# v of block 0 loaded in 1 KB runs and put in token order by 0/1 matrix products, with a new order table

## The chip, the core and the metric

The kernel runs on one NeuronCore of a Trainium2 chip. Five engines work at the same time, each through its own list of instructions in order: TensorE (matrix products; PE in the profile, PEld its weight loads), VectorE (DVE), ScalarE (ACT), GpSimd (POOL) and SyncE (SP), which only issues transfers. Transfers run on 16 DMA engines. TensorE writes to PSUM, eight banks of 128 x 512 fp32 values; the other engines read results from there. The metric is the device time in microseconds. Before the change it is 293.98 us, the median of three runs (293.78 to 295.15).

## The reference

Chunked attention, then a bilinear feed-forward part:

```python
# q, k, v: (8 batches, 8 heads, 576 tokens, 64), chunks of 64 tokens
scores = q_c @ k_c.T / sqrt(64)          # inside each chunk
attn   = softmax(scores)                 # (sum + 1e-9 below)
out    = attn @ v_c
x = out.transpose(0, 2, 1, 3).reshape(4608, 512)
y = ((x @ w_a) * (x @ w_b)) @ w_out      # 512 -> 1536 -> 512
```

Inputs and output are fp32. The kernel computes its products in bf16 and accumulates in fp32.

## The kernel before

The 4608 tokens are nine blocks of 512; a block is two units of 256 tokens. For each unit the kernel loads q, k and v, casts them to bf16, turns q and k so that the head dimension lies on the partitions, forms scores, the exponential E (ScalarE), its sums (products with ones), the inverse of the sums, and the values, and multiplies the two into `xT`, x with features on the partitions. The feed-forward part then streams `xT` past the weights. For block 0 that is `ffn`, 24 groups of four products of 128x512 (L772), each group one tile of 128 hidden features of w_b or w_a. From block 1 on it is `side_group` (L861) and `out_seven` (L1166, and L1004 at the end), which need fewer products through sums and differences of operands.

Block 0 is special, because everything waits for it. Its q and k are loaded by head pairs (`load_pair`): pair m is heads 2m and 2m+1, all 512 tokens, and partition p takes four tokens in a row, so that a run in memory is 4 x 64 x 4 bytes = 1 KB. `cast_pair` casts, `turn_pair` turns a pair's q or k with four products and copies the result to `qkT` so that tokens are in order; `scores_pair`, `sums_pair` and `values_pair` follow. `sums_pair` makes the inverse of the sums with two VectorE reciprocals for pair 1 and with ScalarE's Ln and Exp for the others. v of block 0 is loaded by `load_v0` with tokens on the partitions in order: a run is one head of one token, 256 B. Two loads make a half (256 tokens, all heads), and `cast_v` casts a half to the buffer `vb` in one instruction of 128x1024. `values_pair` reads both `vb` buffers. The same scheme with pairs serves units 2 and 3 (block 1); the later units use loads of another shape and turns by DMA.

The weights w_a and w_b come in pieces of 512 KB (`load_four`), each half of the input features for 512 hidden features, and are cast to `WA` and `WB`. The groups of the first four tiles of each weight are split, so that their first half can start with the first half of the input features (xT of pairs 0 and 1).

The order of all work is written out by hand in a table, `ORDER_OF_ALL`, which `Planner.follow` reads: each word is an engine letter (a TensorE, b ScalarE, c VectorE, d GpSimd, e a DMA issue) with the number of an operation and, behind a colon, the PSUM banks that it takes. A word with f is a filler, one 128x512 product of a zero tile into a free bank (L1474 in the profile). Per engine, instructions stand in the table's order. One extra rule holds for GpSimd: its instruction waits for the last VectorE instruction of a fast kind ahead of it in the table.

The end of the kernel writes the groups' results by DMA; nothing of it is touched except for its place in the table.

Of the kernel before, what the change touches and what calls it, by code (L numbers as in the profile page):

```python
# [85 lines left out]
c113 e0 b1 e2 b3 e4 e8 b5 e6 e9 c48 f0 f1 f2 f3 f4 f5 f6 f7 f0 f1 a49:0 c50 d51 f2 a52:1 d57 f3 f4 a58:2 b7  # L86
d60 e10 e11 f5 a61:3 d66 b62 c53 a54:45 c59 f6 f7 a63:67 e12 b55 b56 a67:0 c68 b64 b65 f1 f2 a93:12 d69 a70:3
b71 f4 f5 f6 a72:45 c94 b73 a86:67 b74 b75 b88 d78 a79:0 b80 f3 f3 f4 a76:3 b77 f5 f1 f4 f5 a81:45 a99:17 b87
c84 c95 d85 a96:03 c97 f6 a90:62 b89 c91 d13 e16 d17 e135 e14 d15 c98 e18 e134 e20 e22 b83 b101 b82 f5 a106:50
b108 a103:74 a110:63 b100 e115 c92 b107 b109 c112 d145 c111 a158:2 a170:0 b102 c105 c104 a152:1 a153:5 a171:3  # L90
a164:6 a165:4 a166 c168 a159:7 a154 b19 a160 a161 c162 e133 e114 a155 d21 c23 c246 b156 c248 c250 a146:6 b147
a172 b123 b174 a173 c175 a188:1 b190 b120 a180:2 a184:6 b186 a167 a176:0 e28 a124:1 b139 a140:3 b141 d142
a143:6 b182 b144 c157 d29 e30 c31 a200:5 c125 c169 e117 d129 a130:1 e116 a121:3 c163 b178 b131 d126 a127:2
b128 a204:4 e136 e24 d148 a149:6 b150 c122 c25 c258 e26 c27 c252 c247 c254 c256 b206 b202 a196:7 a208:03 b210
b209 e137 a227:12 b228 b229 a181:6 c183 c198 a192:4 b194 a185:5 c187 e138 e32 a220:30 a271:12 a177:4 e34 d33
c35 c179 a189:6 c191 d249 e119 e118 c132 a193:7 a205:5 c260 b222 d253 b151 a224:04 b221 b223 c225 c226 d285
b273 b272 b274 a275:36 c276 e36 b37 a201:2 a197:1 c277 c283 c284 c195 a287:0 b288 a289:4 b290 a333:3 c334
a341:6 c207 a336 b337 d251 d255 d257 d286 e44 e38 a338 b339 d39 e263 b45 c199 a331:7 c332 c203 a342 a340:3
b343 a382:5 a351:1 a345 c344 e42 e262 e40 d41 b346 c347 a349:7 b350 a353 b354 a362:2 c363 a355 a359 c360 a357
c358 b43 a364:0 a372:2 b352 c365 a369 d268 e46 c230 a367 b47 c238 c242 a411:6 b370 a376 c377 c378 b368 a373  # L100
d231 d243 c356 e265 e264 b269 a412 b374 a371:3 c375 a384 b413 b385 c233 c232 c239 c241 c234 c244 c240 e214
b383 e213 b218 a423:0 a390 a424 c391 e211 e212 b217 d335 a388 c389 a393:4 a380:7 b381 a426 a427 e216 b428 a400
a398 a431 a395:2 a386 b401 a432 a407 c237 e266 e267 b279 c236 a429:3 d235 c425 b433 c394 c387 e270 b399
a308:04 b310 c396 b408 b309 a404 a430 a443 a320:12 b405 b321 a416 b322 d366 c348 a444 a414 c245 c361 c259 c261
c397 c434 c379 c453 a324:40 c445 e219 a280:12 b323 c325 a446 a447 c326 c448 a402:6 c406 b281 b282 a300:41 b302
b301 b303 e215 d278 a304:20 d435 c392 e292 e312 e291 a403:3 c409 d410 a418 c419 d457 c305 c306 a535:1 a420
c421 c436 c438 b415 b297 a526:4 a587:6 a536 a441:7 b442 a439:2 b440 a519:0 c520 d437 a524 b525 c417 e293 e294
d298 a517:3 a522 b523 c518 a531 b532 a527:0 c533 b537 a528 b529 c530 e311 a561:5 b562 b317 a579:3 a540 a544
a538 c545 c580 a584 c539 a542 c543 c541 e449 e314 e313 b318 a559:0 d422 d463 d521 b585 a577:3 a591 d459 c461
b560 c578 a582 b583 b592 c593 a597:2 c598 d454 d462 d534 d458 a612:4 a586:7 a588 b589 c590 d594 a595:3 b596  # L110
a605 c606 a599 c600 a619 e315 a601 a603 c604 c602 d456 d464 e465 e296 e467 a617 a614:6 a547:0 a548 b618 d455
b620 e316 b327 e299 a328:75 a623 a626 b330 b329 c615 a550 b627 e472 e319 a488:65 b489 b490 e466 c613 c624
a480:47 b482 c549 a638 c639 a640 c641 a551 c552 e295 d546 a622:0 b481 b483 a506:65 a510:37 b508 d307 a484:42
a555 c628 d616 e493 c486 c485 a621:5 c625 c629 c460 b507 e451 e498 e496 e468 a553:2 e494 e469 e452 e501 e471
b509 c512 c511 c630 c631 a753:6 a644 a693:4 a556 b557 e470 a636:7 a642 c643 e495 b477 e492 c645 d575 a554
a634:3 b637 a563 c632 d607 e474 a698 a564 b699 c635 a696 b565 c694 c558 c697 a691:5 a705 d646 c581 c692 d573
c574 a700:0 a701:4 a702 a566 a733:1 b706 c707 b478 b703 a712 e491 e450 b503 e497 b504 a567 c704 e500 a735:5
d633 a718 a716 b713 d608 e475 e476 e502 e473 c568 b487 a709:2 a760:3 c736 a758 c754 c719 b759 a710 b711 d647
d648 d650 a751:6 d609 c717 a714 c734 a756 c752 b757 c715 c720 a761:4 a765 b766 c767 a769:0 a762 a721:6 a771:7
a722 c763 a773 c764 a777 e499 e652 c723 d610 e651 e479 b772 b657 a779 a775 b774 c778 a793 b770 a791 e505  # L120
a668:61 d755 c780 c794 b670 a514:34 a724 a725 a800 b516 b515 a660:14 d768 d708 d611 c649 c792 c776 d781 c695
b669 a680:36 b681 b661 b682 b662 c726 e571 a788:5 c789 a797 b801 a786:3 a729 c787 c798 d513 a664:15 a684:64
b683 c685 c686 a730 b663 a814 a796:3 a812 a795:6 a727:4 a728 e572 e656 e672 e671 b677 c665 c666 a810:1 a825:5
d804 c805 e674 b731 b813 e673 e653 b678 c802 b811 a808:0 a818 c799 d576 d803 a737 a832 a738 a816 e654 b658
c809 c826 c790 c819 d782 c815 c817 c820 c806 a902:5 a830 e570 b739 e655 b833 a827:3 c828 a834:2 a835:7 b831
a836 b837 c732 a839 c840 c841 e676 e675 b687 a900:6 c838 d807 a846 a740 d749 c747 d748 b903 a925:3 a852 c853
a850 c851 a932 b901 a930 c926 c933 d667 d784 b931 b847 a741 c742 a848 c849 a936 a934:7 b937 c938 e679 a865:23
b870 e659 e858 a688:04 b689 b690 a947 c783 d829 c948 a939 e855 a927:1 c928 c940 a935:3 c941 a864:04 d750 b869
a892:62 b896 b895 a951 a943:1 c952 e885 e884 e882 c944 b867 b866 b868 a945:2 a843:6 c946 a949 c950 a844 a953
c954 b845 a962:4 d821 d889 c963 c822 a970:7 a967 c968 a891:05 a914:34 c929 b897 c917 c823 d942 e886 c916 c893  # L130
c978 a965 b966 a874 a875 b876 e887 b920 e856 a960:4 a974 e883 b888 c975 c976 c894 d842 c961 e857 b862 a969:3
a871:0 a872 a879 a971 b972 c973 a984:5 a880 a992 a986 c985 d955 d854 d979 a877:4 a1006 a878 c987 e569 e745
c873 b861 e860 d980 a990 e859 e1059 c993 c991 e746 c1007 a982:1 b983 d981 d898 a1074:0 c824 a1001:7 c1002
a1004 a988 a999:3 c1000 b881 d785 a904 a1008:7 b1005 a1010 a905 a1009:3 b1011 c956 e744 a1013 b1014 c899 a907
a1020 a908 d964 c989 c977 c994 c995 d957 a1103:2 c1012 a1024 d996 b1021 c1015 a1026 c1075 c1104 b906 a1076:1
b1077 d921 c1025 a1108 a1105:6 b1109 a1110 c1027 b1111 c909 a1022 c1023 e890 a1039:27 b1044 c1106 e1030 e1031
e743 e863 a915:34 b918 b1043 b919 a1114 c1115 a1112:5 c1116 a1117 c1118 a1121:7 a1066:63 b1070 b1069 c1122
a1038:24 b1040 a1125 c1126 b1041 b1042 a1129 e1029 e1034 d998 e1032 c1130 e1056 d923 d922 d1003 a1138:3 c1139
e1057 e1058 e1060 c1036 a1127 a1113:6 c1128 a1092:20 b1035 c1016 a1065:45 c1067 a1017:3 a1143 a1123:1 a1018
a1045:4 c1119 b1071 c1095 c1124 c1094 d1062 b1019 b1144 a1131 a1140:0 e912 c1132 a1149 a1046 c1150 e1033 e910  # L140
e1210 e1061 e1235 b1072 e1209 a1048 a1049 b1050 e913 a1147:2 a1145 b1146 c1068 a1164 c1047 c1141 d959 d958
d1156 d997 a1053 e1208 c1157 e1212 c1107 c1159 c1158 c1120 b1063 a1054 b1055 c1165 a1152 b1153 a1148:6 c1154
a1160:5 a1051:4 a1162:0 c1151 b1161 d1028 d924 a1170 c1171 a1168 c1169 a1179:7 a1182 a1078 a1079 a1177:6 a1052
b1163 c1183 a1252:2 a1184 b1185 c1180 c1133 d1142 c1178 d1181 d1155 a1188 c1189 a1186:7 b1080 a1187:6 a1166
a1277:3 a1191 c1073 a1081 a1082 d1136 c1190 c1167 d1172 d1175 b1253 a1254:1 a1202 d1099 d1134 c1192 c1193
a1204 a1200 d1194 e1037 e1064 d1100 b1255 a1282 c1203 b1283 c1278 c1083 c1205 a1198 b1199 c1201 a1284 c1285
a1288 b1289 a1286:7 c1290 a1217:34 a1093:56 b1096 b1221 a1279:0 c1280 b1222 a1291 b1292 a1295:5 a1299 d1206
# [31 lines left out]
def kernel(  # L179
# [1346 lines left out]
```

## Time and profile before

| | |
|---|---|
| median of three runs | 293.98 us |
| span of the profiled execution, first to last instruction | 291.4 us |
| the profiled execution's own time | not listed apart; the median is 2.58 us above its span |
| busy: PE, DVE, ACT, POOL | 285.0, 245.6, 181.5, 175.3 us |
| first feed-forward product of block 0 / block 1 | 16.28 / 42.94 us |

A row of the timeline has the start, the length, the engine, the line, the operation with output and inputs, the count and, in brackets, the idle time ahead of it with what ended it. A row of the busy table has a stretch, its length, each engine's busy time and count, the TensorE clock that the throttle granted, and the DMA share and rate. A row of the waits has who waited for what, the sum in us, the number of times and the longest. L326 is the line of the helper `copy`, so casts and copies are told apart by tile. Many products overlap, so a busy TensorE need not be at its peak.

### The profile page before, as it was taken

Reading aid. Unit: us, or ns where it says so; the run is one execution under the profiler, and the core shown is the slowest. Engines: PE = TensorE matmul, PEld = TensorE weight load, DVE = VectorE, ACT = ScalarE, POOL = GpSimd, SP = SyncE. Lnnn points to the kernel's source line nnn. Section 1 sums busy time; section 2 is a strip of 40 time slices with the busy share of each in tenths; the row PEclk is TensorE's granted clock in tenths of the full one; section 3 lists DMA queues with packets and bytes.
Section 4 is the critical chain, followed back from the end, with each engine's and each line's share of the span. In section 5 each row is a group of like instructions: output and inputs, shape, how many; then the busy total and the mean of one; then the engine's idle time right before and its main releaser. Section 6 shows DMA issues by size and latency. Waiting matters only on the chain.

```text
span 291.4 us, 8635 instructions
## 1 busy us (share of the span) xinstructions
PE 285.0 (98%) x3522; PEld 232.6 (80%) x3522; DVE 245.6 (84%) x432; ACT 181.5 (62%) x308; POOL 175.3 (60%) x168
## 2 busy tenths in 40 slices
PE   8999989999999999999999999999999999999995
PEld 3545448887888888888888888888888888888884
DVE  2758989999897999989998989888997788697893
ACT  1767878978877775795675468525944684333221
POOL 3354248443789389835739694569447764676540
PEclk9999999999999999999999999999999999999999
DMA  7999999999998789939996995939290210003034
GB/s 244 335 395 393 310 282 340 246 216 246 213 213 219 191 175 274 240 75 201 260 259 158 203 277 126 253 88 242 76 219 3 80 69 2 0 2 144 3 133 156
DMA packets 140248, 55.09 MB, mean 189 GB/s; under 512 B 126256, under 2 KB 131504, under 8 KB 140208
## 3 DMA queue, kind: packets, MB, share of 16 engines
q1 hardware_dynamic: 138976, 53.43, 71.8%
q10 hardware_dynamic: 1232, 1.11, 1.1%
q8 instruction: 27, 0.44, 0.7%
q14 instruction: 13, 0.11, 0.1%
HBM read 37.75 MB, written 9.44 MB: 162 GB/s over the span
## 4 chain that ended last, share of the span: by engine, by line
PE 91%; ACT 3%; DVE 2%; DMA 1%; issue 1%; POOL 0%; SPq 0%; POOLq 0%
PE F L861 49%; PE F L1166 24%; PE F L772 6%; PE F L1004 3%; PE F L1474 2%; PE F L635 1%; PE F L645 1%; PE F L492 1%; PE F L673 1%; DMA f<-in_k_dram 1%; ACT inv L697 1%; ACT inv L695 1%; DVE xT L722 0%; POOL wst L821 0%; ACT E L528 0%
## 5 line engine op out<-in xcount | busy, mean ns | idle before, releaser
L326 ACT COPY part<-F 128x512 f32<-128x512 f32 x87 | 50.4, 591 | 49.0 <-PE F L861 32.2
L895 POOL TENSOR_TENSOR AB<-AB,bsb 128x512 bf16<-128x512 bf16 x45 | 51.7, 1156 | 38.7 <-DVE wst L1123 15.5
L899 DVE TENSOR_TENSOR bsb<-F,part 128x512 bf16<-128x512 f32 x72 | 49.0, 685 | 10.4 <-PE F L861 4.9
L326 ACT COPY wst<-F 128x512 f32<-128x512 f32 (+1 forms) x43 | 24.0, 561 | 30.5 <-PE F L861 14.7
L861 PEld LDWEIGHTS <-WB 128*128 128x128 bf16 x384 | 37.3, 98 | 5.2 <-issue 0.5
L861 PEld LDWEIGHTS <-WA 128*128 128x128 bf16 x384 | 37.2, 98 | 4.8 <-issue 0.3
L899 DVE TENSOR_TENSOR AB<-F,part 128x512 bf16<-128x512 f32 x48 | 32.9, 686 | 3.7 <-PE F L861 1.6
L1123 POOL TENSOR_TENSOR wst<-AB 128x512 bf16<-128x512 bf16 x27 | 31.0, 1155 | 7.0 <-PE F L1166 4.7
L861 PEld LDWEIGHTS <-Ta 128*128 128x128 bf16 x288 | 27.9, 98 | 3.9 <-issue 0.5
L861 PEld LDWEIGHTS <-Tb 128*128 128x128 bf16 x288 | 27.4, 98 | 4.4 <-issue 0.9
L1166 PEld LDWEIGHTS <-AB 128*128 128x128 bf16 x288 | 28.0, 98 | 3.4
L1166 PEld LDWEIGHTS <-wst 128*128 128x128 bf16 x288 | 27.8, 98 | 3.4
L861 PE MATMUL F<-wst,Ta 128*128 128x256 bf16 x192 | 28.8, 273 | 0.1
L861 PE MATMUL F<-wst,Tb 128*128 128x256 bf16 x192 | 28.8, 273 | 0.0
L861 PE MATMUL F<-wst,WB 128*128 128x256 bf16 x192 | 28.8, 273 | 0.0
L861 PE MATMUL F<-wst,WA 128*128 128x256 bf16 x192 | 28.8, 273 | 0.0
L861 PE MATMUL F<-xT,WA 128*128 128x256 bf16 x192 | 28.2, 273 | 0.0
L861 PE MATMUL F<-xT,WB 128*128 128x256 bf16 x192 | 28.1, 273 | 0.0
L1166 PE MATMUL F<-WO,AB 128*128 128x256 bf16 x192 | 25.5, 273 | 0.0
L326 DVE COPY part<-F 128x512 f32<-128x512 f32 x33 | 22.4, 684 | 2.7 <-PE F L861 2.0
L326 ACT CAST qkb<-f 128x1024 bf16<-128x1024 f32 (+1 forms) x24 | 23.2, 986 | 0.3 <-DMA f<-in_q_dram 0.3
L1123 POOL TENSOR_TENSOR wst<-wst,AB 128x512 bf16<-128x512 bf16 x16 | 18.4, 1155 | 6.0 <-DVE wst L1123 5.9
(126 smaller groups left out, 551.7 us busy)
## 6 DMA issues: line engine op xcount, KB each, us to landing
f<-in_q_dram SPq DMA_DIRECT2D x32, 256.0 KB, 4.2
f<-in_v_dram SPq DMA_DIRECT2D x32, 256.0 KB, 4.2
f<-in_k_dram SPq DMA_DIRECT2D x28, 256.0 KB, 4.8
out_dram<-osb SPq DMA_DIRECT2D x28, 256.0 KB, 3.5
wst<-in_moe_w_b_dram SPq DMA_DIRECT2D x6, 512.0 KB, 7.8
wst<-in_moe_w_a_dram SPq DMA_DIRECT2D x6, 512.0 KB, 6.9
wst<-in_moe_w_out_dram SPq DMA_DIRECT2D x6, 512.0 KB, 6.8
out_dram<-osb SPq DMA_DIRECT2D x12, 128.0 KB, 2.4
```

The source lines that it names most:

```text
L326: return A.copy(out=out, in_=in_) if e == "act" else ENG[e].tensor_copy(out=out, in_=in_)
L492: T.transpose(turned()[:, r, :], qkb[hu][:, x, mm * 512 + r * 128:mm * 512 + r * 128 + 128], identity)
L635: T.matmul(PS[j][cl * 64:cl * 64 + 64, c:c + 64], chunk_of(u, 1, m, j, 2 * g + cl), chunk_of(u, 0, m, j, 2 * g + cl), start=True, stop=True,)
L645: T.matmul(SU[cl][j * 64:j * 64 + 64, :], ones[cl * 64:cl * 64 + 64, :], E[u % 2][cl * 64:cl * 64 + 64, j, :], start=True, stop=True,)
L772: T.matmul(f_of(b)[:, 0:n].rearrange("p (u t) -> p u t", u=len(us)), w[ft][:, kt, :], x[:, us[0]:us[-1] + 1, kt, :], start=(kt == 0), stop ...
L861: T.matmul(f_of(bank)[:, q * 256:q * 256 + 256], lhs(2 * g + q, kt), rhs[:, kt, :], start=(first and q == 0 and kt == 0), stop=(q == 1 and ...
L895: op(("dve", "pool"), TIMES, lambda e: ENG[e].tensor_tensor(out=dst, in0=dst, in1=b, op=MULT), r=bk, w=key, prio=-300, fast=True)
L899: op("dve", c_dve(512), lambda e: V.tensor_tensor(out=dst, in0=two(f_of(bank)), in1=two(pab[s][i]), op=ADD), r=[("ps", id(bank)), ("part", ...
L1004: T.matmul(f_of(bank)[:, 0:256], lhs[:, i, h], rhs[:, i, :], start=(first and i == 0), stop=(i == NP - 1), skip_group_check=True)
L1123: op(*long_op(hs), lambda e, i=i, x=x, y=y, o_=o_: ENG[e].tensor_tensor(out=SS[i][:, s], in0=x[:, s], in1=y[:, s], op=o_), r=fts + [(name, ...
L1166: T.matmul(f_of(bank)[:, at:at + 256], lhs[:, i, tt * 128:tt * 128 + 128], rhs[:, i, :], start=(first and at == 0 and i == 0), stop=(i == ...
L1474: "fn": lambda e: T.matmul(F[at], zero[:, 0:128], zero, start=True, stop=True),
```

## The change

For block 0 (`PLACED`), `load_v0` loads v as q and k are loaded, by head pairs with four tokens in a row to a partition: a run is 1 KB. Tokens are then not in order: partition p holds tokens 4p to 4p+3. A half is now two head pairs (256 columns of features, all 512 tokens). `place_v` casts each pair of a half to bf16 into an output buffer that is free at that time (`v_rows`), then 16 products with slices of a 0/1 matrix (`picks`) put the tokens in order: group g of 128 tokens lies on the 32 partitions 32g to 32g+31, and the four products r = 0 to 3 of a group, each with 32 rows, accumulate in a bank of PSUM. ScalarE or VectorE copies each of the four banks (128x256) to `vb`. `values_pair` now waits only for the half of v that its pair is in. `picks` is made by GpSimd at the start. v of block 1 is loaded as before.

```diff
+    PLACED = (0,)
+    BY_HALF = (0,)
+    PLACE_CASTS = ("pool", "act", "dve")
...
+    picks = osb[2].rearrange("p t c -> p (t c)").bitcast(BF16)[:, 0:515]
...
     def load_v0(half, K=0):
+        if K in PLACED:
+            for m in (2 * half, 2 * half + 1):
+                mm = m % 2
+                load(
+                    f32[half][2][:, mm * 512:mm * 512 + 512].rearrange("p (h c) -> p h c", h=2),
+                    v[K, 2 * m:2 * m + 2, 0:BLK, :].rearrange("h (p r) d -> p h (r d)", r=4),
+                    [("f32", half, 2, 2 * mm), ("f32", half, 2, 2 * mm + 1)], (256, 42),
+                )
+            return
...
+    def place_v(K, half):
+        rows = v_rows(K, half)
+        for mm in range(2):
+            op(PLACE_CASTS, ..., lambda e, mm=mm: copy(e,
+                rows.rearrange("p (r h d) -> p r h d", r=4, h=4)[:, :, 2 * mm:2 * mm + 2],
+                f32[half][2][:, mm * 512:mm * 512 + 512].rearrange("p (h r d) -> p r h d", h=2, r=4)), ...)
...
+            for r in range(4):
+                for g in range(4):
+                    T.matmul(
+                        f_of(VB[g])[:, half * 256:half * 256 + 256],
+                        picks[32 * g:32 * g + 32, 128 * g + 3 - r:128 * g + 131 - r],
+                        rows[32 * g:32 * g + 32, r * 256:r * 256 + 256],
+                        start=(r == 0), stop=(r == 3), skip_group_check=True,
+                    )
...
+                op(("act", "dve"), (c_act(n), c_dve(n)), lambda e, g=g, c=c: copy(e, vb[g // 2]..., f_of(VB[g])[:, c]), ...)
...
-    cast_v(0, V_CASTS, R0 + 0.4)
-    cast_v(1, V_CASTS, R0 + 0.5)
+    for half in range(2):
+        if 0 in PLACED:
+            place_v(0, half)
+        else:
+            cast_v(half, V_CASTS, R0 + 0.4)
...
+        G.memset(picks, 0.0)
+        G.affine_select(out=picks, in_=picks, pattern=[[-1, 515]], compare_op=not_equal, fill=1.0, base=3, channel_multiplier=4)
```

The whole table `ORDER_OF_ALL` is new: order, engines and banks of all operations. Its start, with seven fillers (f0) ahead of the first turns (a49, a52) where ten stood, is below. Over the table 15 fillers stand where 30 did, the placing products of half 0 are a86 and those of half 1 a93, all four casts of v are GpSimd's (d84, d85, d91, d92), six of the eight copies of placed v are ScalarE's and two are VectorE's; the sums of pair 1 (a105) stand behind the turn of pair 3's q (a76) and the scores of pair 2 (a72). Four groups of block 0's feed-forward part, all on w_a, stand among the first products of block 1, where all 24 groups stood ahead of those; and v of block 1 is issued ahead of the last two pieces of w_a, where it was issued partly behind them.

```diff
-c113 e0 b1 e2 b3 e4 e8 b5 e6 e9 c48 f0 f1 f2 f3 f4 f5 f6 f7 f0 f1 a49:0 c50 d51 f2 a52:1 d57 f3 f4 a58:2 b7
...
+c125 e0 d48 b1 e2 b3 e4 b5 e6 b7 c51 c57 f0 f0 f0 f0 f0 f0 f0 a49:0 b50 e8 a52:1 b53 f2 a58:2 c59 a54:34 b55 b56 d60
+f5 a61:5 b62 d66 f6 a67:6 d69 e9 b68 a98:70 b100 a70:1 c71 a63:23 b64 b65 d75 a76:4 c77 f5 a72:56 b74 b73 a105:02 c107
+d78 a79:1 d84 b99 b80 d85 f3 f3 f3 a86:3465 c90 c88 e10 d91 b87 a81:71 b83 b89 b101 e11 d92 a93:2351 b96 b82 b97 c106
...
```

More of the change, by code (lines that the diff above doesn't have):

```diff
@@ L91 @@
[L91 to L100, printed above, removed]
@@ L590, in values_pair, with vb_keys @@
             o["ahead"] = AHEAD * (1 - hu)
+    def vb_keys(n):
+        return [("vb", n, g, h) for g in range(2) for h in range(2)]
     def cast_v(u, engs, prio):
         cost = {"dve": 0.69, "pool": 1.04, "act": 1.05}
-        op(engs, [cost[e] for e in engs], lambda e: copy(e, vb[u % 2], f32[u % NF32][2]), r=f_keys(u, 2), w=[("vb", u % 2)], prio=prio, fast=True)
+        op(engs, [cost[e] for e in engs], lambda e: copy(e, vb[u % 2], f32[u % NF32][2]), r=f_keys(u, 2), w=vb_keys(u % 2), prio=prio, fast=True)
@@ new lines, in v_rows, with pe @@
+    def v_rows(K, half):
+        return osb[K].rearrange("p t c -> p (t c)").bitcast(BF16)[:, half * 1024:half * 1024 + 1024]
+    placing = {}
+    def place_v(K, half):
+        cost = {"dve": 0.425, "pool": 0.61, "act": 0.62}
+        rows = v_rows(K, half)
+        for mm in range(2):
+            op(PLACE_CASTS, [cost[e] for e in PLACE_CASTS], lambda e, mm=mm: copy(
+                e,
+                rows.rearrange("p (r h d) -> p r h d", r=4, h=4)[:, :, 2 * mm:2 * mm + 2],
+                f32[half][2][:, mm * 512:mm * 512 + 512].rearrange("p (h r d) -> p r h d", h=2, r=4),
+            ), r=[("f32", half, 2, 2 * mm), ("f32", half, 2, 2 * mm + 1)], w=[("osb", K, half, mm)], prio=R0, fast=True)
+        if K in BY_HALF or not half:
+            placing[K] = [P.bank("F") for _ in range(4)]
+            keep.extend(placing[K])
+        VB = placing[K]
+        def pe(e):
+            for r in range(4):
[6 more added lines that the diff above has]
+                    )
+        op("pe", 0.441, pe, r=[("osb", K, half, mm) for mm in range(2)] + [("osb", 2, 0, 0), ("osb", 2, 0, 1)], w=[("ps", id(b)) for b in VB], ps=VB, prio=R0, mode="32")
+        if K in BY_HALF or half:
+            for g in range(4):
+                hs = (half,) if K in BY_HALF else (0, 1)
+                c = slice(256 * hs[0], 256 * hs[-1] + 256)
+                n = 256 * len(hs)
+                op(("act", "dve"), (c_act(n), c_dve(n)), lambda e, g=g, c=c: copy(e, vb[g // 2][:, g % 2 * 512:g % 2 * 512 + 512][:, c], f_of(VB[g])[:, c]),
+                   r=[("ps", id(VB[g]))], w=[("vb", g // 2, g % 2, h) for h in hs], ps=[VB[g]], prio=R0)
@@ L1344, in value_in @@
     def value_in(u):
-        if u < NU:
+        if u in TWO and 1 in PLACED:
+            place_v(1, u % 2)
+        elif u < NU:
             cast_v(u, EARLY_CASTS if u < 8 else CASTS, -60 + u)
```

164 lines of the change are left out of this document (84 added, 80 removed).

## The prediction

> **What bounds the kernel now.** I read the page's busy shares first, then busy time by stretch, then the list of waits of TensorE, and last the start of each engine in order of time.
>
> ```profile
> span 291.4 us, 8635 instructions
> PE 285.0 (98%) x3522; PEld 232.6 (80%) x3522; DVE 245.6 (84%) x432; ACT 181.5 (62%) x308; POOL 175.3 (60%) x168
> ```
> ```profile
> core 0: us, PE busy (x) PEld busy (x) DVE busy (x) ACT busy (x) POOL busy (x), PEclk, DMA share, GB/s
> 0.00:16.28 16.28, 14.53 (x207) 7.43 (x208) 9.02 (x14) 7.98 (x19) 6.97 (x15) 1.00 0.95 298
> 16.28:27.20 10.92, 10.92 (x56) 5.11 (x57) 6.77 (x12) 7.25 (x14) 4.43 (x6) 1.00 1.06 396
> 27.20:42.94 15.74, 14.47 (x211) 6.97 (x209) 14.18 (x24) 13.21 (x22) 5.88 (x8) 1.00 0.96 307
> 42.94:60.00 17.06, 17.06 (x158) 15.19 (x157) 16.52 (x30) 14.29 (x22) 10.44 (x10) 1.00 1.16 283
> 60.00:281.00 221.00, 220.85 (x2834) 191.77 (x2832) 193.97 (x342) 136.78 (x226) 146.47 (x131) 1.00 0.67 156
> ```
> ```profile
> PE F L1474 <- DVE zero L1271: 1.3, 1, 1.3
> PE F L772 <- DVE WA L326: 0.8, 1, 0.8
> PE F L660 <- DVE vb L326: 0.4, 1, 0.4
> ```
> ```profile
> 1.26 4.45 PE L1474 MATMUL F<-zero 128*128 128x512 bf16 x10 [1.26 <-DVE zero L1271]
> ...
> 16.28 1.46 PE L772 MATMUL F<-xT,WB 128*128 128x512 bf16 x6
> ...
> 38.69 1.47 PE L772 MATMUL F<-xT,WA 128*128 128x512 bf16 x6 [0.83 <-DVE WA L326]
> 40.54 0.73 PE L660 MATMUL F<-E,vb 64*64 64x64 bf16 x64 [0.38 <-DVE vb L326]
> 41.21 1.90 PE L772 MATMUL F<-xT,WA 128*128 128x512 bf16 x8
> 42.94 0.60 PE L861 MATMUL F<-xT,WB 128*128 128x256 bf16 x4
> ```
> TensorE sets the time: from 60 to 281 us it is busy 220.85 of 221. The feed-forward part starts at 16.28 (L772), block 1's at 42.94 (L861); between the two TensorE waits 0.8 + 0.4 us. So the change can gain in two places only: the head before 16.28, and those 1.2 us. Much of the head's busy time is filler, products of 128x512 with a zero tile (L1474); the first ten take 0.445 us each. Later products of that size take 0.216: eight pass in 1.90, six in 1.47, 0.43 for two.
>
> What ends the head is VectorE, not TensorE and not a load:
> ```profile
> 10.09 1.76 DVE L551 RECIPROCAL inv<-F 128x256 f32<-128x256 f32 x1
> 11.76 0.63 DVE L326 CAST vb<-f 128x1024 bf16<-128x1024 f32 x1
> 12.31 1.75 DVE L551 RECIPROCAL inv<-F 128x256 f32<-128x256 f32 x1
> 14.58 1.64 DVE L583 TENSOR_TENSOR xT<-F,inv 128x256 bf16<-128x256 f32 x4 [0.53 <-ACT inv L555]
> ```
> Two reciprocals of head pair 1, a cast of v between them, a wait of 0.53 us for ScalarE's inverse, then four products into xT, done at 16.22; the feed-forward part starts 0.06 us later.
>
> **The change part by part.** *The loads.* The two rows below are the packets of 2.8 to 4.5 us, nearly all of 1 KB, and of 9 to 10 us, nearly all of 256 B, which are v's.
> ```profile
> DMA packets 644, 0.62 MB, mean 368 GB/s; under 512 B 34, under 2 KB 644, under 8 KB 644
> ```
> ```profile
> DMA packets 1125, 0.29 MB, mean 288 GB/s; under 512 B 1117, under 2 KB 1125, under 8 KB 1125
> ```
> v of block 0 is 1.05 MB: 3.64 us at 288 GB/s, 2.85 at 368. The transfers behind it start 0.8 us sooner. In SyncE's queue the fourth load of q now stands ahead of all of v, where one piece of v went before it. Further back, a load of q of block 1 moves ahead of the first piece of WA, and v of block 1 (still in 256 B runs) ahead of the last two; what needs those pieces is moved too (below). GpSimd's casts show when q and k landed:
> ```profile
> 0.73 0.20 POOL masks.py:197 MEMSET identity<- 128x128 bf16 x1 [0.29 <-POOLq L1510]
> 1.01 0.29 POOL masks.py:199 TENSOR_SCALAR_AFFINE_SELECT identity<-identity 128x128 bf16<-128x128 bf16 x1
> 4.59 0.61 POOL L326 CAST qkb<-f 128x512 bf16<-128x512 f32 x1 [3.29 <-DVE qkb L326]
> 5.52 1.17 POOL L326 CAST qkb<-f 128x512 bf16<-128x512 f32 x2 [0.32 <-DMA f<-in_q_dram]
> 7.15 1.17 POOL L326 CAST qkb<-f 128x512 bf16<-128x512 f32 x2 [0.46 <-DMA f<-in_q_dram]
> 8.53 0.61 POOL L326 CAST qkb<-f 128x512 bf16<-128x512 f32 x1 [0.21 <-DMA f<-in_k_dram]
> ...
> 14.38 1.04 POOL L326 CAST WB<-wst 128x1024 bf16<-128x1024 f32 x1 [0.88 <-DMA wst<-in_moe_w_b_dram]
> ```
> Pair 2 is there at 7.15. Pair 3 is two more loads, 0.52 MB, at the latest 1.4 us later: 8.5. v follows at 0.71 us a load: 9.2 to 11.4. The first weight was cast from 14.38 to 15.42, before it was needed, and moves ahead: no cost, no gain at the start.
>
> *GpSimd.* New are a memset and a select over 515 columns (the 0/1 matrix). They stand ahead of its first cast, behind the identity's, which end near 1.3; the same two on 128 columns take 0.20 and 0.29 us, so at four times that 2.0 us, to 3.3: covered, since GpSimd's first cast starts at 4.59 and the reciprocals wait for pair 1, cast from 5.52. The matrix and the cast rows lie in output buffers that nothing else writes for some tens of us: no wait. Next come six casts of q and k and four of v in place of one, at 0.61 us. Pair 2 takes 7.15 to 8.3, pair 3 8.5 to 9.7, v 9.7 to 10.9 and 10.9 to 12.1. What queues behind is the first weight's cast, which its load holds until about 13.5 in any case.
>
> *TensorE.* Filler falls from 30 products to 15, one of those late; 32 placing products come in, 16 for each half, of 32 rows and 256 columns. No row of the trace has 32-row tiles. The nearest are those of 64 by 64:
> ```profile
> 31.63 0.71 PE L623 MATMUL F<-qkT 64*64 64x64 bf16 x64
> ```
> ```profile
> 57.52 1.31 PE F L861 x12
> ```
> 64 small products, each with its weight load, pass in 0.71 us, so tiles overlap, loads too. Twelve products of 256 columns on the full array take 1.31 us in the chain of waits, 0.109 each. Full overlap over four row groups makes four such steps of 16: 0.44 us a half. None makes 16 x 0.109 = 1.74. I take 0.55, near full overlap, as these tiles behave.
> [...] No row here shows 32-row tiles.
> Half 0 runs from about 10.9 to 11.5 and half 1 from 12.1 to 12.7.
>
> *VectorE.* Its queue: two casts, three copies of turned q and k, reciprocal, two copies of placed v, reciprocal, four products into xT. The first reciprocal needs the sums of pair 1, and TensorE now forms them behind the scores of pair 2 and the turn of pair 3's q (cast near 9.1): about 10.0, as before. Then 1.75 + 2 x 0.42 (the product of the same 128x256 shape takes 1.64 / 4) + 1.75 + 1.64 = 5.98: xT is ready at 16.0. The cast of v that left (0.63) and the lost wait (0.53) pay for the two copies and leave 0.3.
>
> *ScalarE.* It takes six of the eight copies of placed v, and one more copy of turned q and k, and gives up one cast.
> ```profile
> L528 ACT ACTIVATE E<-F 128x256 bf16<-128x256 f32 x8 | 2.6, 383 | 0.4 <-PE F L518 0.4
> L326 ACT COPY qkT<-F 128x512 bf16<-128x512 bf16 x4 | 2.3, 597 | 4.6 <-PE F L492 4.6
> L555 ACT ACTIVATE inv<-F 128x256 f32<-128x256 f32 x2 | 0.8, 414 | 0.0
> L557 ACT ACTIVATE inv<-inv 128x512 f32<-128x512 f32 x1 | 0.6, 632 | 0.0
> ```
> Up to the last copy of v, which the values of pairs 2 and 3 wait for ahead of the first feed-forward product: 5 x 0.60 + 8 x 0.38 + 4 x 0.41 + 0.63 + 6 x 0.38 (the shape of E) = 10.6 us from its first copy at about 5.3: 15.9, if it never waits and nothing overlaps. Its instructions do overlap (eight E are busy 2.6 us, 0.33 each, not 0.38), which its waits use up. Two sets of values, 16 small products each (0.2), follow: 16.3. ScalarE is now as late as VectorE.
>
> So the head ends at 16.1, not 16.28: **-0.2**. Bounds: half 1 cast at 12.1, placed in 0.44, four copies and the four other ScalarE instructions between them at the overlapped 0.33, two sets of values: 15.6; if pair 3 lands at 8.2, without v's piece in front of it, 15.3: -1.0. With 1.74 us a half: half 0 ends at 12.6, half 1, behind the scores of pair 3 (0.3), at 14.7; then the same copies and values: 17.7, +1.4.
>
> *Behind the head.* The new order takes four groups of feed-forward products of block 0 (four of 0.216 us each, 3.45 us) out of the stretch before 42.94 and puts them among the first products of block 1. Those wait for the last pieces of WA, the waits of 0.8 and 0.4: **-1.2** if nothing follows. What is late next is VectorE: in the two stretches from 27.2 to 60 it is free 1.56 + 0.54 = 2.1 us of 32.8. To take the same work 1.4 us sooner leaves 0.7, and the first products of block 1 need xT of block 1 about 4.5 us sooner than now. I give back **+0.5** of the 1.2 (bounds 0 and 1.2, and beyond in a rival below).
>
> *The rest.* Same products; a handful of operations change between GpSimd, ScalarE and VectorE, seven more on VectorE, which from 60 to 281 us is busy 193.97 of 221. **0**.
>
> Sum: -0.2 - 1.2 + 0.5 = -0.9: a span of 290.5. The median time, 293.98, stands 2.58 above the span of this one profiled execution, whose own time is not listed apart; I keep that: **293.1 us**.
>
> **The rivals.**
> *The clock (slower).* Filler kept TensorE dense; of the old head's busy 14.53 us filler is 10 x 0.445 + 20 x 0.216 = 8.8, the turns, scores, sums and values 5.7. The new head has 5.7, placing 1.1 and, behind the first seven fillers (to 4.4 us), seven more (1.5): 8.3 us of work in 11.7. If TensorE is at half rate when the feed-forward part starts, each product of 512 columns costs 0.43, not 0.216. For it: the rate went up here only after ten unbroken products. Against: the longest idle stretch in my walk, ahead of the last values, is some 1.5 us, and after the idle 0.83 us at 38.69 six products pass in 1.47, at full rate. Price: the first ten products ran 4.45 us at half rate; as long again from 16.1 on loses 2.2, half as long 1.1: 294.2 to 295.3; with the head slowed too (1 us) 296.3, middle 295.2. By itself it makes the time slower by over 0.5% from 4.7 us at half rate on.
> [...]
> *VectorE becomes the bound between 27 and 60 us (no gain, or slower).* For it: 2.1 us free of 32.8. Against: much of the free time lies in the two waits that go. Price: the 1.2 stay, and of the 4.5 us by which xT must come sooner up to 4.5 - 2.1 = 2.4 are waited for: 293.8 to 296.2, middle 295.0.
> *The head shortens (faster).* If sums and casts run ahead of my walk, 15.3 and no give-back: -1.0 - 1.2: 291.8. For it: pair 3 lands sooner. Against: two reciprocals still stand in line.
> *The loads are hidden anyway.* That is in the forecast: 0.8 us of transfer becomes 0.2.
>
> **How the numbers follow.** Forecast 0.45 (own range 292.2 to 294.2); clock 0.19; VectorE 0.17; shorter head 0.19. 291.4 to 296.4 leaves out less than 2 in 10. About 0.5%, 1.5 us, is what a measurement of this kernel tells from no change: faster (under 292.5) is the short head and 0.08 of the forecast, 0.27; slower (over 295.5) is about half of clock and VectorE and a little for stalls in the new order, 0.25; the same 0.48.
>
> **What would show it.** The first feed-forward product at 16.1 behind the fourth product into xT; 16 placing products in about 0.55 us; 1 KB packets at 368 GB/s up to 11 us; no wait for WA near 38; products of 0.216 us right from the start of the feed-forward part. Wrong: 0.43 us there, TensorE idle for VectorE between 37 and 60, or a head that ends before 15.5 or after 17.

## The result, and the profile after

The changed kernel takes 309.37 us, the median of five runs (307.76 to 311.49), beside 293.96 us (293.04 to 295.15, five runs) for the kernel before on the same chip: 1.0517 times as long, interval 1.047 to 1.0564. The forecast was 293.1 us in a range of 291.4 to 296.4. The change makes the kernel slower by 15.4 us, well outside the range.

The profiled execution took 307.76 us, the shortest of the five, with a span of 306.0 (before 291.4): 14.6 us to find. Where do they lie? The busy table by stretch answers that at once. First the kernel before:

```profile
core 0: us, PE busy (x) PEld busy (x) DVE busy (x) ACT busy (x) POOL busy (x), PEclk, DMA share, GB/s
0.00:16.00 16.00, 14.27 (x197) 7.19 (x201) 8.80 (x14) 7.72 (x18) 6.69 (x15) 1.00 0.95 296
16.00:43.00 27.00, 25.71 (x293) 12.37 (x281) 21.23 (x37) 20.72 (x36) 10.66 (x13) 1.00 1.01 344
43.00:60.00 17.00, 17.00 (x158) 15.14 (x157) 16.46 (x29) 14.29 (x22) 10.38 (x10) 1.00 1.16 282
60.00:100.00 40.00, 39.85 (x596) 33.75 (x594) 35.66 (x65) 30.16 (x49) 26.65 (x24) 1.00 0.94 219
100.00:150.00 50.00, 50.00 (x663) 43.25 (x664) 46.53 (x79) 36.96 (x58) 33.70 (x30) 1.00 0.94 206
```

The changed kernel, the same stretches and the next one:

```profile
0.00:16.00 16.00, 13.26 (x227) 7.20 (x228) 9.11 (x16) 10.77 (x29) 9.34 (x20) 1.00 0.92 331
16.00:43.00 27.00, 26.84 (x289) 14.72 (x288) 25.40 (x47) 20.69 (x35) 9.94 (x11) 1.00 1.01 350
43.00:60.00 17.00, 15.66 (x132) 12.74 (x131) 16.47 (x30) 12.97 (x20) 9.50 (x9) 1.00 0.99 234
60.00:100.00 40.00, 36.72 (x563) 30.98 (x563) 33.30 (x56) 28.54 (x46) 24.84 (x23) 1.00 1.00 212
100.00:150.00 50.00, 43.32 (x484) 36.05 (x483) 40.92 (x69) 26.57 (x43) 28.48 (x26) 0.93 1.07 228
150.00:200.00 50.00, 48.83 (x681) 42.14 (x679) 43.38 (x74) 32.61 (x54) 34.06 (x31) 1.00 0.82 190
```

Up to 43 us the changed kernel is ahead: TensorE is busy 26.84 of 27 us where it was 25.71. From 43 us on it has holes: 1.34 + 3.28 + 6.68 + 1.17 = 12.5 us idle up to 200 us. And between 100 and 150 us the mean granted clock is 0.93, not 1.00. Over the whole span it is 0.989 in this execution and 0.971 to 0.983 in the other four, a lower clock than this trace shows; where in the span, is not known.

TensorE's rows in the timeline of the changed kernel show the head and the worst hole (start, length, engine, line, operation, count, idle time ahead of it with what ended it):

```profile
10.88 0.62 PE L630 MATMUL F<-osb,osb 32*128 32x256 bf16 x16
11.96 0.87 PE L630 MATMUL F<-osb,osb 32*128 32x256 bf16 x16 [0.21 <-POOL osb L326]
15.84 1.89 PE L822 MATMUL F<-xT,WB 128*128 128x512 bf16 x8
...
37.80 0.60 PE L911 MATMUL F<-xT,WB 128*128 128x256 bf16 x4
...
141.44 0.60 PE L911 MATMUL F<-xT,WB 128*128 128x256 bf16 x4 [3.66 <-DVE bsb L949]
144.24 1.01 PE L911 MATMUL F<-wst,Ta 128*128 128x256 bf16 x4 [1.50 <-POOL wst L871]
```

The head is as forecast. The placing products take 0.62 and 0.87 us a half; the feed-forward part starts at 15.84 (forecast 16.1, before 16.28), eight products in 1.89 us, at a granted clock of 1.00; block 1's first product stands at 37.80, where it was 42.94. Of these 5.1 us, 3.5 are the four groups of block 0 that have moved behind it (16 products of 0.216 us), 0.4 the head, and 1.2 the two waits that are gone. Inside the head the forecast holds too: placing starts at 10.88 and 11.96 us (forecast 10.9 and 12.1), and the 1 KB packets between 9 and 10 us pass at 387 GB/s (forecast 368). The hole at 137.8 to 144.2 has VectorE and GpSimd as its last releasers, but neither is the cause. GpSimd's own rows:

```profile
137.53 1.04 POOL L326 CAST qkb<-f 128x1024 bf16<-128x1024 f32 x1 [8.08 <-DMA f<-in_q_dram]
138.51 1.04 POOL L326 CAST vb<-f 128x1024 bf16<-128x1024 f32 x1
139.51 3.39 POOL L945 TENSOR_TENSOR AB<-AB,bsb 128x512 bf16<-128x512 bf16 x3
```

A cast of q waits 8.08 us for its load, and the three products AB behind it in GpSimd's queue wait with it; VectorE waits 5.98 us for them, and TensorE 3.66 us for VectorE. The list of waits of the changed kernel between 43 and 155 us has this in many places (who waits for what, sum in us, times, longest):

```profile
POOL qkb L326 <- DMA f<-in_q_dram: 12.5, 2, 8.1
POOL vb L326 <- DMA f<-in_v_dram: 7.2, 2, 4.9
ACT qkb L326 <- DMA qkT<-qkb: 6.3, 1, 6.3
ACT qkb L326 <- DMA f<-in_q_dram: 3.5, 3, 2.3
ACT qkb L326 <- DMA f<-in_k_dram: 2.0, 3, 1.1
DVE vb L326 <- DMA f<-in_v_dram: 1.1, 1, 1.1
```

Together 32.6 us in which a cast waits for a transfer. In the kernel before no cast waits for DMA in this stretch (two weight loads of TensorE do, 0.2 us each). The chain that ended last says it in one line, changed kernel (before: PE 91%, DMA 1%):

```profile
PE 59%; DMA 17%; DVE 7%; SPq 7%; issue 5%; POOL 3%; ACT 2%; ACTq 0%; DVEq 0%; POOLq 0%
```

This points away from v's placement, and to the question why the casts of the later units stand waiting for loads.

### The profile page after: what moved, and what is told of

It reads as the page before. It is cut to its first block, busy times and chain, and to the rows that moved or that the text cites. A ratio compares the mean times of both kernels' runs of the same rounds, so it can differ in the third digit from the quotient of the medians.

```text
span 306.0 us, 8675 instructions
## 1 busy us (share of the span) xinstructions
PE 287.4 (94%) x3539; PEld 234.0 (76%) x3539; DVE 254.9 (83%) x443; ACT 181.0 (59%) x309; POOL 174.5 (57%) x168
## 4 chain that ended last, share of the span: by engine, by line
PE 59%; DMA 17%; DVE 7%; SPq 7%; issue 5%; POOL 3%; ACT 2%; ACTq 0%; DVEq 0%; POOLq 0%
PE F L911 34%; PE F L1216 17%; DMA f<-in_k_dram 5%; SPq L355 5%; DMA f<-in_v_dram 3%; PE F L1054 3%; DMA wst<-in_moe_w_b_dram 3%; DMA wst<-in_moe_w_a_dram 3%; DMA qkT<-qkb 2%; POOL AB L945 1%; DVE bsb L949 1%; DVE AB L949 1%; SPq L653 1%; DMA f<-in_q_dram 1%; PE F L685 1%
## 5 line engine op out<-in xcount | busy, mean ns | idle before, releaser
L326 ACT COPY part<-F 128x512 f32<-128x512 f32 x85 | 49.2, 590 | 48.9 <-PE F L911 28.1
L326 ACT COPY wst<-F 128x512 f32<-128x512 f32 (+1 forms) x40 | 22.5, 564 | 28.9 <-PE F L1216 18.5
L1173 POOL TENSOR_TENSOR wst<-AB 128x512 bf16<-128x512 bf16 x25 | 28.7, 1156 | 17.5 <-DVE AB L945 7.2
L911 PEld LDWEIGHTS <-Tb 128*128 128x128 bf16 x288 | 28.3, 99 | 6.5 <-issue 2.4
L326 ACT CAST qkb<-f 128x1024 bf16<-128x1024 f32 (+1 forms) x25 | 24.8, 1013 | 13.6 <-DMA qkT<-qkb 6.9
L326 POOL CAST qkb<-f 128x512 bf16<-128x512 f32 (+1 forms) x14 | 10.8, 781 | 30.9 <-DMA f<-in_q_dram 14.6
L326 DVE COPY part<-F 128x512 f32<-128x512 f32 x35 | 23.6, 683 | 2.4 <-PE F L911 1.2
L1216 PE MATMUL F<-WO,AB 128*128 128x256 bf16 x192 | 24.7, 273 | 0.0
```

The costliest lines, as they stand in the source:

```text
L326: return A.copy(out=out, in_=in_) if e == "act" else ENG[e].tensor_copy(out=out, in_=in_)
L911: T.matmul(f_of(bank)[:, q * 256:q * 256 + 256], lhs(2 * g + q, kt), rhs[:, kt, :], start=(first and q == 0 and kt == 0), stop=(q == 1 and ...
L1173: op(*long_op(hs), lambda e, i=i, x=x, y=y, o_=o_: ENG[e].tensor_tensor(out=SS[i][:, s], in0=x[:, s], in1=y[:, s], op=o_), r=fts + [(name, ...
L1216: T.matmul(f_of(bank)[:, at:at + 256], lhs[:, i, tt * 128:tt * 128 + 128], rhs[:, i, :], start=(first and at == 0 and i == 0), stop=(i == ...
```

## The experiments

Two theories. *Order:* the loss is made by the new table behind the head. *Placement:* it is made by the placing steps and the earlier head, whatever the order behind. Words of the table are quoted as they stand in it; the times of the kernel before beside these runs were 293.8 to 294.2 us.

### 1 and 2: the table without the placement, the placement without the table

The new table with v of block 0 loaded and cast as before:

```diff
-d84 ... d85 f3 f3 f3 a86:3465 c90 c88 e10 d91 b87 a81:71 b83 b89 b101 e11 d92 a93:2351 b96 b82 b97
+d84 f3 f3 f3 e10 a81:71 b83 b89 e11 d85 b82
```

> The new table of order, engines and banks stays word for word, except that v of block 0 is loaded, cast and used the old way: the placing products, their eight copies and the GpSimd casts of its rows are left out, and everything is still computed. Order theory: the loss of 15.4 us comes from the new order behind the head, so this kernel loses it too: 304 to 310 us, with TensorE idle and half-rate stretches between 60 and 155 us. Placement theory: the loss needs the placing steps and the head that they make, so without them the time is back at 292 to 296 us.

The old table with the placing steps put in at one spot (`BY_HALF = ()`: both halves of v in one go):

```diff
-d78 a79:0 b80 f3 f3 f4 a76:3 b77 f5 f1 f4 f5 a81:45
+d78 d84 d85 d87 d88 a79:0 b80 f3 f3 f4 a76:3 b77 a86:0137 a89 c90 b91 c92 b93 a81:45
```

> The mirror of the run before: v of block 0 is loaded in 1 KB runs and placed by 0/1 matmuls, the placing steps are put into the old table at one spot (four filler products leave, two halves of eight casts and copies come in), and every other step keeps its old place, engine and bank. Order theory: 293 to 296 us; the head ends within 1 us of 16.3 and TensorE is busy from 60 us on as before. Placement theory: most of the loss is here, 300 us or more.

Measured: 310.55 us (ratio 1.0561, 1.0528 to 1.0594) without the placement; 295.28 us (1.0039, 1.0019 to 1.0059) with it in the old table. The first stands 0.55 us above the order theory's range, the second inside it: the table alone carries a loss of this size, and v's placement costs little. The first kernel's head is 1.7 us longer than the changed kernel's (feed-forward part at 17.51, with a granted clock of 0.59 from 15.3 to 18.7), so the two losses are not made of the same parts throughout; but between 43 and 200 us its TensorE is idle 11.7 us, for 12.5 in the changed kernel. One part of the expectation missed: in the second kernel the feed-forward part starts at 19.43, not within 1 us of 16.3 (all of v is placed in one go, and the last values wait 0.88 us for an inverse). Of these 3.2 us only 1.5 are left in the time; the waits of 0.8 and 0.4 us near 38 are gone, and TensorE is busy from 60 us on as before.

### 3: the new head, the old order behind

The changed kernel; behind step 225, block 1's first product (a299), the remaining words go in the old relative order:

```diff
 c237 c238 f7 a299:7
-a301:6 b302 a363:2 d263 b300 c289 b210 d297
+c210 b206 e34 c35 a205:1 a217:6 d265 d297
```

> The changed kernel with its own table up to block 1's first product (the first 225 steps), and behind that all steps in the relative order of the old table. Order theory, with the fault behind block 1's first product: 291 to 295 us, since the head ends at 15.9 and block 1's first product starts 3 us or more sooner than 42.94 or the same work is done. Rival: the earlier head takes products ahead of their loads (DMA share is 0.94 already between 60 and 150 us in the kernel before), so that TensorE waits whatever the order: 298 us or more, with waits for DMA between 60 and 155 us.

Measured 294.97 us (1.004, 1.0025 to 1.0056): the order theory holds here too. No cast waits for DMA between 43 and 155 us. What the head gains goes in small waits: 0.35 us at 35.8, 0.68 at 39.6, 0.67 at 55.7 and 1.01 at 90.2.

### 4: the new table with the old queue of SyncE

```diff
-e26 e148 e146 e147 e28 e30 e150 e149 e131 e130 e32 ...
+e30 e129 e128 e148 e24 e26 e149 e150 e32 e34 e131 e130 ...
```

> The changed kernel with one thing of its table undone: SyncE's 192 loads, transposes and stores go in the relative order of the old table (172 of them change their place in its queue); TensorE's and VectorE's orders stay the new ones word for word, and ScalarE's and GpSimd's too but for 21 and 8 steps that had to step aside for a load that now comes later. SyncE theory: the loss is made by SyncE's new order (a load or transpose late in its queue), so most of it goes: 293 to 298 us. Rival, the order on the computing engines: 304 us or more, since TensorE and GpSimd ask in an order that the old queue does not serve.

Measured 366.22 us (1.2487): neither theory gave a number like this. In this kernel ScalarE's casts wait 42.9 us for loads of q, and GpSimd's 31.8 for q and k. The order of the loads and that of the computing engines belong together: with the old queue the loads come still later than the new order asks for them. The run doesn't tell which of the two is at fault in the new table.

### 5: the one cast that starves TensorE

```diff
-d816 ... d873 ... d679 ... d767 d815 ... d793 d818
+d816 ... d767 d815 ... d793 d873 d679 d818
```

> The changed kernel with two steps of GpSimd's queue moved: the casts of q and v of a later unit, of which the first waits 8.08 us for its load up to 137.53, go behind the three products AB that stood behind them; no other engine's order changes. If that one cast in line is what starves TensorE there: its waits of 3.66 and 1.50 us near 141 and 144 go, and with them the 6.83 us at half rate (3.4 us of work), 300 to 303 us against 309.4 for the changed kernel. Rival, the loads are late as a whole there and TensorE waits for the next late tile instead: 306 us or more.

Measured 306.08 us (1.0408, 1.0353 to 1.0463), 3.3 us less than the changed kernel and 3 us above the range expected of the one cast: the rival's value. The wait of 3.66 us and the half-rate stretch near 142 are gone (the clock is 1.00 from 100 to 150 us, where it was 0.93), but the next late things come up: 1.72 us at 140.9, 0.91 at 143.3, and at 162.8 a wait of 2.08 us for ScalarE, with a granted clock of 0.51 behind it (162.9 to 166.3). Casts still wait for loads and transposes (5.9 + 3.7 + 2.3 + 2.1 + 1.5 = 15.5 us). It isn't one misplaced step.

### 6 and 7: which part of the table

The first 600 steps (to about 100 us) old and the rest new, and the mirror of that:

```diff
 c643 e495 b477 e492
-c645 d575 a554 a634:3 b637
+e497 e491 e473 e476 e475 d607 c581 a554
```

> The kernel before, with the first 600 steps of its table (up to about 100 us) as they were, and every step behind them in the relative order of the new table. Local theory (each stretch of the new order loses its own time): the losses of 100 to 200 us come back, 6.7 us idle, 3.4 at half rate and 1.2 idle, so some 305 us, 301 to 308. Rival, the later stalls are the late effect of what goes wrong before 100 us: 293 to 297 us.

```diff
 b516 b636 c586 a646:3
-a634:0 a648:2 e514 e480 e486 c637
+e461 d476 e477 e479 b639 a650 c651
```

> The mirror: the changed kernel with the first 600 steps of its own table (up to about 100 us) and the old relative order behind them. Local theory: only the idle time of TensorE between 43 and 100 us stays, 1.3 + 3.3 us, less what the shorter head gains: 296 to 299 us, at full clock behind 100 us. Rival, the late start feeds stalls behind 100 us whatever the order there: 303 us or more.

Measured: 307.06 us (1.0422, 1.0375 to 1.047) with the new order behind, and 299.77 us (1.019, 1.0148 to 1.0232) with the new order ahead. The first is as the local theory has it: the sound order up to 100 us does not help what comes behind. The second is 0.8 us above the range: TensorE waits 2.60 us for a transpose up to 88.8, and the granted clock is 0.54 from 88.4 to 91.8, which the forecast left out. The losses of the two, 13.3 and 6.0 us, add up to more than the 15.4 of the whole; each kernel has a seam between two orders, which may cost something of its own (not shown). So the new order loses time in both parts, not at one place.

### 8: the cut made sooner

The new table up to step 100, the old order behind it:

```diff
 a164:1 c124 e16 d17
-a170:4 a171:7 e14 a165:5 e20 b137 c15 a172
+e147 e14 d15 e18 e146 e20 e22 d157
```

> The changed kernel with its own table for the first 100 steps alone (the head of block 0, up to the first two feed-forward products), the old relative order behind: the cut of the third run, made sooner. Order theory: the head's gain of 0.4 us is kept, the waits of 0.8 and 0.4 us near 38 stay as before, and the waits of 0.7 and 1.0 us near 56 and 90 that the third run showed go: 292.5 to 294.2 us, 0.7 us or more under the third run. Rival, any lead that the head makes is lost to waits behind it: 294.5 us or more, as in the third run (294.97).

Measured 292.41 us (0.9952, 0.9936 to 0.9969): faster than both kernels, if only by half a per cent. The head's gain can be kept. The waits of 0.8 and 0.4 us near 38, which were expected to stay, are gone; two new ones, 0.78 at 20.05 and 0.71 at 31.33, stand in their place.

### 9 and 10: the same orders with less to load

If the casts are late because the loads are, smaller loads must cure the new order without a word of its table changed:

```diff
-t[p:p + rows, g * 512:(g + 1) * 512].rearrange("p (h d) -> p h d", h=H),
-src[b, :, s0:s0 + rows, :].transpose([1, 0, 2]),
+t[p:p + rows, g * 512:g * 512 + (512 if u < 4 else 256)].rearrange("p (h d) -> p h d", d=64),
+src[b, 0:(H if u < 4 else H // 2), s0:s0 + rows, :].transpose([1, 0, 2]),
```

> The changed kernel, its table word for word, with less to load: from unit 4 on, each load of q, k and v in 256 B runs carries the first half of its heads and leaves the other half of the tile as the unit before it left it, so that part of the computation works on old numbers. All other steps stay. If the new order loses its time because the casts stand closer behind their loads than the DMA queues can keep up with (GpSimd, ScalarE and VectorE wait 32.6 us for DMA between 43 and 155 us), these waits shrink by half or more and the time falls to 294 to 299 us. Rival, the new order of TensorE's and VectorE's work loses the time by itself: 303 us or more.

> The control of the run before: the kernel before with the same halved loads (half of the heads of q, k and v from unit 4 on stay old numbers). TensorE is busy there from 60 us on and no cast of these loads waits for DMA, so both theories expect 292 to 294.5 us. Below 291 us it would mean that loads bind the old order too.

Both kernels leave out half of the heads of these loads, so they serve for the time alone. Measured: the new order falls to 292.12 us (0.9935, 0.9907 to 0.9964), from 309.37, and below the 294 to 299 that were expected; the control, the old order, stays at 293.89 us (1.0001, 0.998 to 1.0022). Busy table of the new order with halved loads, from 43 us on:

```profile
16.00:43.00 27.00, 27.00 (x292) 14.74 (x291) 25.60 (x48) 20.89 (x37) 9.78 (x10) 1.00 1.02 348
43.00:60.00 17.00, 17.00 (x146) 14.09 (x145) 16.47 (x30) 13.90 (x21) 9.42 (x10) 1.00 0.73 183
60.00:100.00 40.00, 40.00 (x599) 34.16 (x598) 38.05 (x67) 31.62 (x51) 26.55 (x25) 1.00 0.70 152
100.00:150.00 50.00, 49.89 (x689) 42.81 (x687) 47.12 (x82) 35.87 (x58) 34.24 (x32) 1.00 0.84 188
```

TensorE's 12.5 us of holes are down to 0.11 up to 200 us, and the clock is 1.00 throughout. The only wait of a cast for DMA that is left between 43 and 155 us is 0.3 us. So the order of TensorE's and VectorE's work does not lose the time: with smaller loads it is better than the old one by 1.8 us. What it asks of the loads is what full loads did not meet (32.6 us of waits in the changed kernel). Between 43 and 150 us the DMA share falls from between 0.99 and 1.07 to between 0.70 and 0.84. The old order runs at 0.94 and more, too, but no cast of it waits for DMA between 43 and 155 us, and halved loads bring it nothing.

What the new order asks can be counted, since no cast of these two kernels waits more than 0.3 us for its load or transpose there. SyncE's loads of q, k and v issued between 43 and 155 us (count; shortest, median and longest issue in ns; start of the first and the last), the new order and then the old:

```profile
L355 SPq DMA_DIRECT2D f<-in_q_dram x32: 378/584/1924, 43.9 to 154.0; - x32
L355 SPq DMA_DIRECT2D f<-in_k_dram x31: 368/506/762, 43.4 to 153.4; - x31
L355 SPq DMA_DIRECT2D f<-in_v_dram x28: 368/506/1656, 50.0 to 152.8; - x28
```
```profile
L355 SPq DMA_DIRECT2D f<-in_k_dram x25: 368/535/1787, 43.2 to 148.6; - x25
L355 SPq DMA_DIRECT2D f<-in_v_dram x24: 367/595/1591, 51.4 to 143.6; - x24
L355 SPq DMA_DIRECT2D f<-in_q_dram x22: 499/578/1984, 48.8 to 140.5; - x22
```

The new order wants 91 loads in a stretch in which the old one wants 71: it works on q and k of the later units sooner, and its last load of q starts at 154.0 us, the old order's at 197.3. With full loads the changed kernel gets 77 issued in the same stretch: of the 20 loads more, six.

One thing the pair doesn't separate. Halving the loads also eases SyncE's queue: between 43 and 155 us a transpose holds it for 3.00 us in the median in the changed kernel, 1.96 with halved loads and 1.91 in the kernel before; and from 100 to 150 us its issues fill 45 of the 50 us, where they fill 35 with halved loads and 39 in the kernel before. A load of the changed kernel lands 4.1 us (median) from its issue there, about as before (4.0), so it is the issue that comes late. Whether the rate of the DMA engines or the line in SyncE's queue is the limit is not shown.

### 11: a cut between the two

```diff
 b151 c187 b143 d138
-a152:6 a139:0 b140 a188:5 b202 a220:74
+e147 e146 d157 a158:6 b159 b202 a188:0 e28
```

> The best kernel so far (new table for its first 100 steps, old order behind: 292.41 us) with the cut made at 150 steps. It has waits of 0.78 us at 20.05 (VectorE's cast of an output) and 0.71 at 31.33 (ScalarE's copy of qkT) that the cut at 225 steps did not have. If they belong to the seam, the cut at 150 loses them and the time is 291.0 to 292.3 us. Rival, every step taken further from the new table brings in waits for later casts, as the cut at 225 did: 293 to 295 us.

Measured 291.8 us (0.9908, 0.9876 to 0.994), the best of all: 0.9% faster than the kernel before. The waits at 20 and 31 us are gone, and TensorE is busy from 16 us to 200 without a hole, with no cast waiting for DMA from 43 to 155 us.

### 12: loads ahead in SyncE's queue

The changed kernel with 83 loads moved up past transposes and stores, here e278, e325, e228 and e326 past the transpose e282:

```diff
-e276 e274 e42 e275 e277 e225 e223 e224 e227 e226 e282 e231 e279 e278 e325 e228 e326 e306 e304
+e276 e274 e275 e277 e225 e223 e224 e227 e226 e279 e278 e42 e325 e228 e326 e282 e306 e304 e305
```

> The changed kernel with 83 of SyncE's loads of q, k and v moved up in its queue, past transposes and stores that wait there for other engines, as far as the step that frees their buffer; the loads keep their order among themselves, and no other engine's order changes. If the loads are late because they stand behind waiting transposes and stores in SyncE's queue, TensorE's stalls go: 293 to 300 us. Rival, the buffers (two of each kind, freed by the casts) or the DMA queues' rate make them late, and a transpose that now comes later costs as much: 305 us or more.

Measured 351.22 us (1.1934, 1.1866 to 1.2002). The rival's side, and far beyond it: SyncE now waits at its loads for ScalarE to free buffers (32.7 us for casts of v, 21.6 for casts of q and k), and the transposes behind them come late (TensorE waits 16.3 us for them). So moving the loads up in the table does not make room for them: the queue then stands still at a load whose buffer isn't free. The run doesn't tell whether buffers or transfers were the limit in the changed kernel.

## Why the prediction was wrong

- *The loads of v and the head* were right: first feed-forward product at 15.84 for 16.1. The placing products, 0.55 us forecast within 0.44 to 1.74, took 0.62 and 0.87; the second is 0.3 us longer than forecast, and the head ended sooner than forecast all the same.
- *Behind the head, -1.2*: right in its mechanism. The wait for `WA` is gone from the list of the changed kernel, and with halved loads TensorE is busy 27.00 of 27 us between 16 and 43. *The +0.5 given back to VectorE* was not needed there: with halved loads VectorE stands at 16.47 of 17 us between 43 and 60 and TensorE doesn't wait.
- *"The rest. Same products ... 0"* is the step that failed, and with it the time by some 16 us (309.37 for 293.1). It counted products and operations per engine, and these did stay nearly the same (VectorE has eleven operations more in the table, not seven, which did not matter). What it left out is that the new table puts every load, transpose and cast of the later blocks in another order, one that asks for 91 loads of q, k and v between 43 and 155 us instead of 71 (runs 9 and 10), and that the kernel before already has a DMA share of 1.16 from 43 to 60 us and of 0.94 from 60 to 150: the prediction quoted the 1.16 and drew nothing from it. The changed kernel does not move fewer bytes. By the rates of the busy tables times their lengths it has moved 14.7 MB at 43 us (before 14.0), 18.7 at 60 (18.8), 27.2 at 100 (27.6) and 38.6 at 150 (37.9). It is its order that needs more by then, and that starts sooner: block 1's first product stands 5.1 us ahead of where it was.
- *The rivals.* VectorE as the bound between 27 and 60 us is not what the runs show: the one long hole of TensorE there, 1.57 us up to 60.24, ends with a copy of ScalarE's; between 43 and 60 us VectorE is as busy as before (16.47 us for 16.46), and with halved loads, at the same 16.47, TensorE does not wait. The clock rival named the wrong place. There is no half rate at the start of the feed-forward part in the profiled execution of the changed kernel, where its clock is 1.00, but 6.83 us of half rate from 142.5 us on, 3.4 us of work lost, behind the hole of 3.66 us; run 5, which is without that hole, has a clock of 1.00 there. None of the rivals was "a transfer that arrives too late behind the head", which is what the runs show.
- *Sum*: the forecast's other terms were near. With loads out of the way the changed kernel takes 292.12 us, 1.8 us under its control, where -0.9 was forecast; without the +0.5 given back it would have been -1.4. It was the arithmetic of a kernel whose loads arrive.

What stays open: which words of the new table would have to move, and whether the DMA engines' rate or SyncE's queue makes the loads late. The order of the loads and the order that asks for them can't be exchanged one by one (run 4), moving loads up alone makes it worse (run 12), and the cuts show only that both long parts of the table lose some.

## What to carry to other kernels

When a change comes with a new order of everything, the order is the change: price it by how many loads it asks for in each stretch and how far each stands ahead of its first reader, and not by counting operations. Here a DMA share of 0.94 and more stood beside a TensorE busy 39.85 of 40 and 50.00 of 50 us (60 to 100 and 100 to 150 us before the change), and an order that was better for TensorE by 1.8 us lost some 17 to its loads (309.37 for 292.12). Halving the loads is a cheap run that tells whether they bind. And a new table can be taken in part: cut it where its gain ends (here after 150 of 1,687 steps) and keep the old order behind, which gave 291.8 us where the whole table gave 309.4.

## What was not expected of the hardware

At the hole of 3.66 us TensorE lost more than its length: behind it the granted clock was 0.50 for 6.83 us. The changed kernel around the hole at 137.8 to 141.4 us (stretch, length, busy times, clock, DMA share and rate):

```profile
138.00:142.00 4.00, 0.56 (x6) 0.50 (x6) 1.30 (x3) 2.55 (x4) 4.00 (x5) 1.00 1.16 263
142.00:146.00 4.00, 2.50 (x16) 1.71 (x14) 3.16 (x5) 2.41 (x4) 3.58 (x4) 0.56 0.76 199
146.00:150.00 4.00, 4.00 (x24) 2.87 (x23) 2.67 (x4) 0.59 (x1) 3.10 (x3) 0.58 1.12 254
150.00:154.00 4.00, 4.00 (x96) 3.44 (x94) 2.87 (x6) 2.96 (x6) 0.00 (x0) 1.00 0.92 211
```

The granted clock is half from 142.5 to 149.3 us; half of these 6.83 us is 3.4 us of work. In the 3.41 us ahead of that TensorE was busy 1.08 us. Here are the 3.4 us ahead of a fall in run 7 (a wait of 2.60 us for a transpose; clock 0.54 from 88.4 to 91.8), the same in run 5 (2.08 us for ScalarE; clock 0.51 from 162.9 to 166.3), and a stretch of run 5 behind which the clock stayed up (1.72 us for ScalarE; clock 1.00 up to 150 us):

```profile
85.30:88.70 3.40, 0.94 (x9) 0.59 (x7) 1.56 (x3) 0.58 (x1) 3.40 (x5) 1.00 0.71 158
```
```profile
159.50:162.90 3.40, 1.32 (x13) 1.04 (x11) 3.06 (x5) 2.61 (x4) 2.90 (x4) 1.00 1.16 325
```
```profile
139.10:142.50 3.40, 1.54 (x13) 1.17 (x12) 0.69 (x1) 3.40 (x5) 3.40 (x4) 1.00 1.07 273
```

TensorE was busy 0.94 and 1.32 of 3.4 us ahead of a fall, and 1.54 where none came: 2.46 and 2.08 us idle, beside 1.86. Whether the idle time decides, and from where on, these few stretches do not show.

One fall comes without such a hole (the longest wait there is 0.23 us). The profile of run 11 has it in the head:

```profile
12.27:15.67 3.40, 2.88 (x80) 1.61 (x74) 3.34 (x7) 3.40 (x12) 1.76 (x3) 1.00 1.06 401
15.67:19.07 3.40, 3.40 (x38) 1.75 (x39) 3.07 (x8) 2.10 (x5) 1.04 (x1) 0.50 1.06 402
```

TensorE is busy 2.88 of 3.4 us ahead of the fall, but with the small products of the head alone (tiles of 32 or 64 rows); the clock is then 0.50 from 15.67 to 19.07, and the first eight feed-forward products take 3.13 us instead of 1.89. The changed kernel has the same small products and no fall; in the 3.41 us up to 16.22, with 0.4 us of feed-forward products and four turns of 128 x 128 inside, TensorE is busy 2.90 us, and the clock stays at 1.00:

```profile
12.81:16.22 3.41, 2.90 (x79) 1.74 (x79) 3.20 (x7) 3.38 (x12) 1.56 (x3) 1.00 1.05 401
```

So what the prediction's rival of the clock feared happened in the head of run 11, at a cost of 1.2 us (3.13 for 1.89). Two of its six executions have a mean clock of 0.994 and four of 1.00; what tells the two from the four, and whether the size of the tiles is the reason, is not shown.
